# Block-local attention with routed experts: eight token rows to a partition, shared window rows copied inside SBUF, block means from sums and a product

## The chip, the cores and the metric

One core of a Trainium2 chip runs the whole program. The metric is the device time of one execution in microseconds; of several executions the median is taken. A profiled execution gives the trace: engine by engine, what ran when, what it waited for, and what the DMA engines moved.

## The reference

Two layers in sequence. The first is an attention over 4 x 8 heads, 768 tokens and 64 channels. Each query sees the keys less than 16 positions away, and 24 block summaries: for each block of 32 tokens the channelwise maximum of its keys and the mean of its values.

```python
k_sum = k.reshape(B, H, nb, block, D).max(axis=3)        # block = 32, nb = 24
v_sum = v.reshape(B, H, nb, block, D).mean(axis=3)
mask_l = np.abs(pos[:, None] - pos[None, :]) < window    # window = 16
scores_s = scale * np.einsum('bhsd,bhnd->bhsn', q, k_sum) + np.log(block)
scores_l_m = np.where(mask_l, scores_l, -1000000000.0)
scores_all = np.concatenate([scores_l_m, scores_s], axis=-1)
scores_all = scores_all - np.max(scores_all, axis=-1, keepdims=True)
a = np.exp(scores_all)
a = a / (np.sum(a, axis=-1, keepdims=True) + 1e-09)
v_all = np.concatenate([v, v_sum], axis=2)
return np.matmul(a, v_all).astype(np.float32)
```

The second layer sends each of the 3072 tokens, as a row of 512 channels, to the one of 8 experts with the largest gate logit: `relu(x @ w1[e]) @ w2[e]`, with 1024 hidden channels, times the gate's probability and a sigmoid. All inputs and outputs are float32.

## The kernel before, in words

**Attention tiles.** The work goes through 4 batches; a batch has 6 token tiles of 128 tokens, each of them two query blocks of 64 (`NB` = 12 in a batch), and a tile has two halves of the heads. That makes 48 stages `(b, tok, g)`. In a stage:

- `scores` multiplies each block's queries, for two heads at once, with a row of 120 columns (`W`): 48 keys before and in the block, 24 key maxima, 48 more keys. VectorE adds the mask and takes the minimum (L329), ScalarE the exponential (L331).
- `turn_p` transposes the weights on TensorE (L339) and copies them out.
- `values` multiplies them with a *window* `VW` of 120 rows (L350): 48 value rows, the 24 value means, 48 value rows, for all 8 heads, with a column of ones for the denominator. VectorE divides (L360), and POOL stores the tile to `x_dr`.
- `turn_x`, `logits`, `turn_logits` compute the gates; `route` (twice per batch) gives every token a place in its expert's list, with chains of small VectorE instructions (L402 to L446) and six scatters by POOL.

There are 9 window buffers (`VR`), used in turn.

**Preparation.** Queries and keys come in thirds of a batch: `load` brings 256 tokens of 8 heads, two token rows to a partition, so that a packet is 512 B. `reorder` copies the third so that a pair of heads is contiguous (L211 on VectorE, at the start also L209 on ScalarE); `transposed` turns it on TensorE (L273); `prep_k` and `prep_q` copy it from PSUM into `KT` and `QT` (L192), and `prep_k` takes the key maxima (L287), which `k_sum` spreads into the score rows (L296). `KT` holds a whole batch, twice; `QT` holds a third of one, twice, zeroed at the start by VectorE (L174), as half of it must be zero.

Value means: `load_vm` reads the values once more, 32 rows of 64 channels to a partition; `v_sum` adds them up (in the first batch L230 on VectorE, later L237 and L241 on POOL), `mean` scales them and POOL stores them to DRAM, from where `load_vsum` brings them into each window (L262). `load_vw` brings the value rows of two windows, in 256 B packets (L255, L256); neighbouring windows both load the 32 rows that they share.

**Order.** All of these loads go through SP's queue in the order that the code gives; the windows are loaded two token tiles ahead. The other engines' queues are ordered by a planner, which keeps to the order of the code where operands are ready. Before the first stage stand the memsets of the windows on POOL (L182), the first batch's keys, two thirds of its queries, its means and three token tiles' windows.

**Experts.** In the last batch the early experts' weights are fetched (L731), split into a high and a low part by ScalarE and VectorE (L733, L734), and multiplied in three products (L763 to L765, L852 to L854). Tokens are gathered from the lists by POOL (L712). This part begins near 200 us and runs to the end.

Of the kernel before, what the change touches and what calls it, by code (L numbers as in the profile page):

```python
# [20 lines left out]
P = 128  # L21
# [9 lines left out]
BUFS = {"sm": 4, "mn": 4, "pr": 4, "pT": 3, "xs": 3, "den": 3, "xT": 2, "ls": 2, "rawk": 3, "rawq": 2, "natk": 2, "natq": 2}  # L31
# [4 lines left out]
ON_DVE = ("p1", "lt", "ls")  # L36
RE = "vavavvv"
# [28 lines left out]
C_END = C_SEL + 2 * E  # L66


def constants():
# [20 lines left out]
    c[:, C_SEL:C_SEL + 2 * E] = p[:, None] % 32 == np.arange(2 * E)[None, :]  # L90
    return c
# [77 lines left out]
def attention(tc, const, sa, sb, st, ps, dr, q, k, v, id_sb, c_sb, wg_sb, x_dr, l_dr, rt, late_work):  # L169
    nc = tc.nc  # L170
    QT, KT, VW = [], [], []
# [8 lines left out]
    for i in range(VR):  # L180
        t = sb.tile([W, H, VP], F32, name=f"vw{i}", tag=f"vw{i}", bufs=1)
        nc.gpsimd.memset(t, 0.0)  # L182
        nc.gpsimd.memset(t[:, :, D:D + 1], 1.0)
        VW.append(t)
    def evac(what, dst, src, scale=None):
# [8 lines left out]
    vs_dr = dr.tile([B, H, NS, D], F32, name="vs_dr")  # L194
    raws, nat = {}, {}

    def load(kind, src, b, u):
        raw = (sa if kind == "k" else sb).tile([P, H, 2, D], F32, name=f"raw_{kind}{b}{u}", tag=f"raw{kind}",
                                               bufs=BUFS["raw" + kind])
        nc.sync.dma_start(  # L200
            raw.rearrange("p h j d -> p h (j d)"),
            src[b, :, 256 * u:256 * (u + 1), :].rearrange("h (p j) d -> p h (j d)", j=2))
        raws[kind, b, u] = raw

    def reorder(kind, b, u, engine="v"):
        t = (sa if kind == "k" else sb).tile([P, 2, H, D], F32, name=f"nat_{kind}{b}{u}", tag=f"nat{kind}", bufs=BUFS["nat" + kind])
        r = raws.pop((kind, b, u)).rearrange("p h j d -> p j h d")
        if engine == "a":
            nc.scalar.activation(t, r, AF.Copy)  # L209
        else:  # L210
            {"v": nc.vector, "p": nc.gpsimd}[engine].tensor_copy(t, r)  # L211
        nat[kind, b, u] = t

    vm = {}

    def load_vm(b, *os):
        for o in os:
            t = sa.tile([96, 32 * D], F32, name=f"vm{b}{o}", tag="vm", bufs=2)
            nc.sync.dma_start(t, v[b, 4 * o:4 * o + 4].rearrange("g (n s) d -> (g n) (s d)", n=NS))
# [720 lines left out]
```

## Time and profile before

| what | value |
|---|---|
| median of 3 runs (lowest to highest) | 564.43 us (563.89 to 564.97) |
| the profiled execution: time, span | 563.66 us, 561.8 us |
| busy: TensorE, VectorE, ScalarE, POOL | 500.7, 395.9, 339.1, 193.1 us |
| mean granted TensorE clock | 0.949 |
| DMA | 117.63 MB in 116799 packets, 53598 of them under 512 B |
| instructions | 12246 |

The span is what the trace covers, from the first to the last instruction; the time of the execution is 1.9 us longer. Lines such as L321 are lines of the kernel; `out<-in` are the program's names for what is written and read. An engine's busy time is an average over the attention and the experts, which have different limits. A number in brackets behind an instruction of the timeline is the idle time of its engine before it, and what ended it; "SPq" and "POOLq" are the queues of SP and POOL. Clock and DMA share are shown with 1.00 as full; the DMA share is the mean over 16 engines.

### The profile page before, as it was taken

The page shows a single profiled execution, that of the slowest core. Times are in us where ns is not written, and L with a number is a line of the kernel's source. Part 1 is how long each engine was busy: PE and PEld are TensorE (multiplying, and loading weights), DVE is VectorE, ACT ScalarE, POOL GpSimd, SP SyncE. Part 2 cuts the span into 40 slices and gives each one's busy share as a digit, 9 for nine tenths or more (in the row PEclk, how much of TensorE's full clock was granted, in tenths as well). Part 3 has the DMA queues.
Part 4 walks back from the last instruction along what each step waited for, and adds up shares of the span by engine and source line. Part 5 has one row for each costly group of instructions (what it writes and reads, how often), then busy time and mean ns, then how long its engine had stood idle before and what let it go on. Part 6 is the DMA issues. An engine that isn't in the chain of part 4 may idle for free. (4 is left out here: it accounts for less than half of the span.)

```text
span 561.8 us, 12246 instructions
## 1 busy us (share of the span) xinstructions
PE 500.7 (89%) x3880; PEld 436.5 (78%) x3880; DVE 395.9 (70%) x1210; ACT 339.1 (60%) x752; POOL 193.1 (34%) x222
## 2 busy tenths in 40 slices
PE   6498998988979789985999999999999999987990
PEld 5497786767768678874989989899898998975770
DVE  8878798759838857952767665776656666666892
ACT  4386786675749747442656554665555655547881
POOL 6036145445541420337643625415113031130111
PEclk8599998998979979997999999999999999998996
DMA  9979999999764874159667485774856737439790
GB/s 233 232 186 251 235 241 250 115 219 232 163 138 120 247 253 150 65 162 317 211 225 272 151 282 185 236 277 139 300 181 232 269 128 264 168 114 332 252 322 26
DMA packets 116799, 117.63 MB, mean 209 GB/s; under 512 B 53598, under 2 KB 78462, under 8 KB 115952
## 3 DMA queue, kind: packets, MB, share of 16 engines
q1 hardware_dynamic: 107584, 97.02, 61.3%
q0 software_dynamic: 9136, 19.69, 11.5%
q8 instruction: 34, 0.56, 0.5%
q14 instruction: 45, 0.37, 0.2%
HBM read 105.50 MB, written 13.79 MB: 212 GB/s over the span
## 5 line engine op out<-in xcount | busy, mean ns | idle before, releaser
L764 PE MATMUL hp<-xhl,w1h 128*128 128x256 f32 x384 | 109.0, 285 | 0.0
L765 PE MATMUL hp<-xhl,w1l 128*128 128x256 f32 x384 | 108.8, 284 | 0.0
L763 PE MATMUL hp<-xhl,w1h 128*128 128x256 f32 x384 | 108.4, 286 | 0.0
L733 ACT ACTIVATE w2h<-raw 128x512 fp32r<-128x512 f32 x104 | 64.7, 629 | 60.5 <-PE yp L854 27.7
L734 DVE TENSOR_TENSOR w2l<-raw,w2h 128x512 fp32r<-128x512 f32 x104 | 70.5, 689 | 35.2 <-ACT w2h L733 34.2
L852 PE MATMUL yp<-w2h,hh 128*128 128x512 f32 x216 | 87.3, 404 | 0.1
L853 PE MATMUL yp<-w2l,hh 128*128 128x512 f32 x216 | 85.4, 395 | 0.0
L854 PE MATMUL yp<-w2h,hl 128*128 128x512 f32 x216 | 85.2, 396 | 0.1
L331 ACT ACTIVATE pr<-sm,mn 128x120 f32<-128x120 f32 x192 | 62.1, 387 | 26.1 <-DVE mn L329 25.8
L763 PEld LDWEIGHTS hp<-xhl,w1h 128*128 128x128 f32 x384 | 73.7, 193 | 2.0 <-DVE w1l L734 0.4
L712 POOL DMA_INDIRECT xg<-x_dr,lst x28 | 32.3, 1152 | 124.5 <-PE xp L745 106.1
L764 PEld LDWEIGHTS hp<-xhl,w1h 128*128 128x128 f32 x384 | 74.1, 193 | 1.2 <-DVE xhl L748 0.2
L765 PEld LDWEIGHTS hp<-xhl,w1l 128*128 128x128 f32 x384 | 74.1, 193 | 0.0
L766 ACT ACTIVATE hh<-hp 128x256 fp32r<-128x256 f32 x96 | 36.5, 381 | 59.1 <-PE hp L765 57.0
L734 DVE TENSOR_TENSOR w1l<-raw,w1h 128x512 fp32r<-128x512 f32 x104 | 66.2, 690 | 7.3 <-ACT w1h L733 6.2
L767 DVE SCALAR_TENSOR_TENSOR hl<-hp,hh 128x256 fp32r<-128x256 f32 x96 | 39.6, 421 | 44.8 <-ACT hh L766 44.7
L321 PE MATMUL sp<-kt,qt 128*128 128x120 f32 x384 | 58.7, 301 | 7.9 <-DVE kt L296 7.0
L733 ACT ACTIVATE w1h<-raw 128x512 fp32r<-128x512 f32 x104 | 58.2, 621 | 6.9 <-DMA raw<-in_moe_w_dram 6.5
L321 PEld LDWEIGHTS sp<-kt,qt 128*128 128x128 f32 x384 | 53.8, 215 | 10.4 <-issue 8.3
L329 DVE CUSTOM_DVE_ANT_0 sm<-sp,c_sb 128x120 f32<-128x120 f32 x192 | 42.9, 277 | 14.6 <-PE sp L321 13.1
L854 PEld LDWEIGHTS yp<-w2h,hl 128*128 128x128 f32 x216 | 40.7, 189 | 9.5 <-DVE hl L823 0.5
L852 PEld LDWEIGHTS yp<-w2h,hh 128*128 128x128 f32 x216 | 41.2, 191 | 8.6 <-ACT hh L822 0.5
(285 smaller groups left out, 906.5 us busy)
## 6 DMA issues: line engine op xcount, KB each, us to landing
raw<-in_moe_w_dram SPq DMA_DIRECT2D x208, 256.0 KB
vw<-in_v_dram SPq DMA_DIRECT2D x88, 96.0 KB
raw_k<-in_k_dram SPq DMA_DIRECT2D x12, 512.0 KB
raw_q<-in_q_dram SPq DMA_DIRECT2D x12, 512.0 KB
vm<-in_v_dram SPq DMA_DIRECT2D x8, 768.0 KB
x_dr<-xs POOLq DMA_DIRECT2D x24, 256.0 KB, 5.8
vw<-vs_dr SPq DMA_DIRECT2D x36, 48.0 KB
vw<-in_v_dram SPq DMA_DIRECT2D x8, 64.0 KB
```

The source lines that it names most:

```text
L321: nc.tensor.matmul(sp[:, 2 * x + y, 0:W], lhsT=qt[:, 2 * g + x, li, :], rhs=kt[:, 2 * g + x, blk * KW:blk * KW + W], start=True, stop=True)
L329: nc.vector.tensor_tensor_reduce(out=sm[:, c, :], in0=sp[:, c, 0:W], in1=c_sb[:, m:m + W], scale=1.0, scalar=3.0e38, op0=ALU.add, op1=ALU. ...
L331: nc.scalar.activation(pr[:, c, :], sm[:, c, :], AF.Exp, bias=mn[:, c:c + 1], scale=-1.0)
L733: nc.scalar.activation(hi, raw, AF.Copy)
L734: nc.vector.tensor_tensor(lo, raw, hi.bitcast(F32), ALU.subtract)
L763: nc.tensor.matmul(hp, lhsT=w_h[:, fs], rhs=self.xh[:, c, :], start=c == 0, stop=False)
L764: nc.tensor.matmul(hp, lhsT=w_h[:, fs], rhs=self.xl[:, c, :], start=False, stop=False)
L765: nc.tensor.matmul(hp, lhsT=w_l[:, fs], rhs=self.xh[:, c, :], start=False, stop=c == NC - 1)
L767: nc.vector.scalar_tensor_tensor(hl[:, j, :], hp, 0.0, hh[:, j, :].bitcast(F32), ALU.max, ALU.subtract)
L852: nc.tensor.matmul(y, lhsT=hh[:, j, tk], rhs=w_h, start=j == 0, stop=False)
L853: nc.tensor.matmul(y, lhsT=hh[:, j, tk], rhs=w_l, start=False, stop=False)
L854: nc.tensor.matmul(y, lhsT=hl[:, j, tk], rhs=w_h, start=False, stop=j == NF - 1)
```

## The change

A unit is now one kind (key, query or value) of one pair of heads, all 768 tokens, eight token rows to each of 96 partitions: 12 units in a batch, 2 KB to a packet. Units are loaded five ahead of the stage and reordered two ahead, from the second batch on always by POOL. `QT` holds a whole batch, twice, and POOL zeroes its halves. Means: a unit of values is added up over its eight rows (three additions), and a product with a constant matrix `C_MEAN` adds four partitions and scales; the result stays in SBUF (`VS`). A window loads only the rows that its left neighbour does not hold; the shared 32 rows and the means are copied inside SBUF by `share_vw`, one token tile ahead. Key maxima are taken in two halves of a unit and joined where they are written into the score rows. The experts' code is the same. The last part of the diff, from `if g == 0` on, stands in the loop over the stages.

```diff
-BUFS = {"sm": 4, "mn": 4, "pr": 4, "pT": 3, "xs": 3, "den": 3, "xT": 2, "ls": 2, "rawk": 3, "rawq": 2, "natk": 2, "natq": 2}
+BUFS = {"sm": 4, "mn": 4, "pr": 4, "pT": 3, "xs": 3, "den": 3, "xT": 2, "ls": 2, "raw": 7, "nat": 4}
-ON_DVE = ("p1", "lt", "ls")
-RE = "vavavvv"
+ON_DVE = ("p1", "lt", "ls", "q11")
+T8 = 8
+G8 = S // T8
+RE = "vapvavvapvav"
+LOAD_AT, REORDER_AT = 5, 2
...
+    c[:, C_MEAN:C_MEAN + NS] = (p[:, None] // 4 == np.arange(NS)[None, :]) / 32.0
...
-        t = sb.tile([P, HP, 4, P], F32, name=f"qt{i}", tag=f"qt{i}", bufs=1)
-        nc.vector.memset(t, 0.0)
+        t = (sa, sb)[i].tile([P, HP, NB, P], F32, name=f"qt{i}", tag=f"qt{i}", bufs=1)
+        nc.gpsimd.memset(t[0:64, :, :, 64:P], 0.0)
+        nc.gpsimd.memset(t[64:P, :, :, 0:64], 0.0)
...
+    def load(kind, b, hp):
+        t = sa.tile([G8, 2, T8, D], F32, name=f"raw_{kind}{b}{hp}", tag="raw", bufs=BUFS["raw"])
+        nc.sync.dma_start(t.rearrange("p h j d -> p h (j d)"),
+                          {"k": k, "q": q, "v": v}[kind][b, 2 * hp:2 * hp + 2].rearrange("h (p j) d -> p h (j d)", j=T8))
+    def reorder(kind, b, hp, engine):
+        if kind == "v":
+            t = raw.rearrange("p h j d -> p h (j d)")
+            n = T8 * D
+            while n > D:
+                n //= 2
+                {"v": nc.vector, "p": nc.gpsimd}[engine].tensor_tensor(t[:, :, 0:n], t[:, :, 0:n], t[:, :, n:2 * n], ALU.add)
+        else:
+            t = sa.tile([G8, T8, 2, D], F32, name=f"nat_{kind}{b}{hp}", tag="nat", bufs=BUFS["nat"])
+            r = raw.rearrange("p h j d -> p j h d")
+            if engine == "a":
+                nc.scalar.activation(t, r, AF.Copy)
+            else:
+                {"v": nc.vector, "p": nc.gpsimd}[engine].tensor_copy(t, r)
+    def v_mean(b, hp):
+        mp = ps.tile([NS, 2, D], F32, name=f"vm{b}{hp}", tag="TR", bufs=PB["TR"])
+        nc.tensor.matmul(mp, lhsT=c_sb[0:G8, C_MEAN:C_MEAN + NS], rhs=nat.pop(("v", b, hp))[:, :, 0:D], start=True, stop=True)
+        evac("vs", VS[b % 2][:, 2 * hp:2 * hp + 2, 0:D], mp)
     def load_vw(b, tok):
-            lo = PAD if blk == 0 else 0
+            lo = PAD if blk == 0 else 2 * PAD
-    def load_vsum(b, tok):
+    def share_vw(b, tok):
         for blk in (2 * tok, 2 * tok + 1):
+            if blk:
+                nc.sync.dma_start(window(b, blk)[0:2 * PAD], window(b, blk - 1)[W - 2 * PAD:W])
             if blk < VR:
-                nc.sync.dma_start(VW[(NB * b + blk) % VR][LW:LW + NS, :, 0:D], vs_dr[b].rearrange("h n d -> n h d"))
+                nc.sync.dma_start(window(b, blk)[LW:LW + NS], VS[b % 2])
     def transposed(kind, b, hp, half):
+        for j in range(4):
+            nc.tensor.transpose(pt[:, j, :], t[:, 4 * half + j, :], id_sb[0:G8, 0:G8])
     def prep_k(b, hp, half):
+        for f in range(2):
+            d = kt[:, hp, PAD + 4 * half + 56 * f:PAD + 4 * half + 56 * f + (NB - 1) * KW]
...
+            evac(f"k{f}{half}", d, src[:, :, :, f, :])
+        nc.vector.tensor_reduce(out=km[b][:, hp, half, :], in_=pt.rearrange("p j (n s) -> p n s j", s=4), axis=AX.XY, op=ALU.max)
+        if half == 1:
...
+            nc.vector.tensor_tensor(own, m[0], m[1], ALU.max)
     def prep_q(b, hp, half):
+        for side in range(2):
...
+            evac(f"q{side}{half}", d, pt[r], -SCALE)
...
+    units = [(kind, b, hp) for b in range(B) for hp in range(HP) for kind in ("vkq" if b else "kqv")]
+    NU = 3 * HP
+    for i, u in enumerate(units[:NU]):
+        load(*u)
+        if i == 3:
+            load_vw(0, 0)
+    for i, (kind, b, hp) in enumerate(units[:NU]):
+        reorder(kind, b, hp, RE[i])
+        if kind == "v":
+            v_mean(b, hp)
+        else:
+            for half in range(2):
+                (prep_k if kind == "k" else prep_q)(b, hp, half)
     load_vw(0, 1)
+    share_vw(0, 0)
+    for u in units[NU:NU + LOAD_AT]:
+        load(*u)
+    for u in units[NU:NU + REORDER_AT]:
+        reorder(*u, "p")
...
         if g == 0:
+            if tok + 2 < TB or more:
+                load_vw(*divmod(b * TB + tok + 2, TB))
+            if tok + 1 < TB or more:
+                share_vw(*divmod(b * TB + tok + 1, TB))
+        for u in units[i + NU + LOAD_AT:i + NU + LOAD_AT + 1]:
+            load(*u)
+        for u in units[i + NU + REORDER_AT:i + NU + REORDER_AT + 1]:
+            second.append(lambda u=u: reorder(*u, "p"))
+        if more:
+            hp, x = divmod(step, 3)
+            if x < 2:
+                second.append(lambda: prep_k(b + 1, hp, x))
+            if x > 0:
+                second.append(lambda: prep_q(b + 1, hp, x - 1))
+            if x == 0:
+                second.append(lambda: v_mean(b + 1, hp))
```

More of the change, by code (lines that the diff above doesn't have):

```diff
@@ L184, in attention @@
         VW.append(t)
+    for i in range(2):
+        t = sb.tile([NS, H, VP], F32, name=f"vs{i}", tag=f"vs{i}", bufs=1)
+        nc.gpsimd.memset(t, 0.0)
+        nc.gpsimd.memset(t[:, :, D:D + 1], 1.0)
+        VS.append(t)
     def evac(what, dst, src, scale=None):
@@ L205, in reorder @@
[L205 to L209, printed above, removed]
-        else:
[L211 to L219, printed above, removed]
-            vm[b, o] = t
```

156 lines of the change are left out of this document (29 added, 127 removed).

## The prediction

> **What bounds the kernel now.** I read the page first, for engines and DMA, then the busy time by stretches.
>
> ```profile
> span 561.8 us, 12246 instructions
> PE 500.7 (89%) x3880; PEld 436.5 (78%) x3880; DVE 395.9 (70%) x1210; ACT 339.1 (60%) x752; POOL 193.1 (34%) x222
> DMA  9979999999764874159667485774856737439790
> GB/s 233 232 186 251 235 241 250 115 219 232 163 138 120 247 253 150 65 162 317 211 225 272 151 282 185 236 277 139 300 181 232 269 128 264 168 114 332 252 322 26
> DMA packets 116799, 117.63 MB, mean 209 GB/s; under 512 B 53598, under 2 KB 78462, under 8 KB 115952
> ```
>
> The share of busy TensorE time (89%) is an average over two stages. [...] The chain of waits reaches back only to 503 us, so it says nothing of the attention stage, the only one that is edited. So I cut that stage where the normalised outputs (L360) of a batch end:
>
> ```profile
> 26.00:65.00 39.00, 36.48 (x417) 31.90 (x416) 32.19 (x150) 29.44 (x78) 15.75 (x18) 0.95 0.93 219
> 65.00:108.50 43.50, 40.23 (x452) 34.04 (x451) 36.28 (x183) 31.34 (x85) 21.04 (x24) 0.96 1.00 204
> 108.50:158.80 50.30, 40.84 (x463) 34.26 (x461) 37.81 (x205) 32.00 (x86) 20.63 (x23) 0.97 1.03 202
> 158.80:210.40 51.60, 45.92 (x467) 39.15 (x468) 36.08 (x186) 35.20 (x89) 19.20 (x23) 0.87 0.66 192
> ```
>
> Columns: stretch, length, busy time and count of PE, PEld, DVE, ACT, POOL, granted clock, DMA share, GB/s. TensorE is busy for 40 to 41 us in the second and in the third batch, but the third takes 7 us longer, with DMA at its fullest. Nothing else is as busy as TensorE, so the stage is TensorE work plus holes. The largest hole lies between batches three and four:
>
> ```profile
> 154.00:168.00 14.00, 9.86 (x66) 8.77 (x64) 4.68 (x26) 5.64 (x14) 6.20 (x9) 0.76 0.69 145
> 168.00:182.00 14.00, 14.00 (x174) 12.57 (x171) 12.22 (x87) 13.31 (x41) 3.11 (x4) 1.00 0.41 109
> ...
> DVE nat_q L211 <- DMA raw_q<-in_q_dram: 6.3, 2, 4.0
> PE pv L350 <- DMA vw<-in_v_dram: 0.8, 1, 0.8
> ...
> 157.79 0.69 DVE L211 COPY nat_q<-raw_q 128x1024 f32<-128x1024 f32 x1 [3.98 <-DMA raw_q<-in_q_dram]
> 159.21 0.66 PE L369 MATMUL xtr<-id_sb,xs 128*128 128x128 f32 x4 [3.58 <-DVE ls L188]
> 163.06 2.75 PE L321 MATMUL sp<-kt,qt 128*128 128x120 f32 x12
> ```
>
> VectorE waits 3.98 us for queries; behind that copy stand the logits copy and TensorE, idle for 3.58 us. TensorE then runs at a lower granted clock (0.76 in this slice): 12 score matmuls take 2.75 us. A slice that holds 66 matmuls instead of 174 has lost 14 x (1 - 66/174) = 8.7 us.
>
> **The change, part by part.** The profiled execution took 563.66 us for its 561.8 us span; the median of the three runs is 564.43, 0.77 higher.
>
> *1. Loads, DMA waits.* Each partition row of a query or key load grows from 512 B to 2 KB, the 32 rows that two windows share come by a copy inside SBUF, 2304 B a row instead of eight times 256 B, and the means no longer go out to DRAM and back. Loads run five units ahead. I let the late query loads go: 8.7 us, of the other 2.3 of the 6.3 I count 1, and 0.8 for the window: -10.5. Ends: -7.1, if only the waits themselves go (6.3 + 0.8), though a wait that is hidden later gives back less, so -5; and -14, if the third batch also comes to the second's length (50.3 - 43.5 = 6.8, beside the 7 or so behind it). What is late next is the order of TensorE's queue, since it is busy for 40 of 43.5 us already.
>
> *2. The start.* Rows of the first 34 us, and prices:
>
> ```profile
> 1.21 2.62 SPq L200 DMA_DIRECT2D raw_k<-in_k_dram  x3
> 3.15 3.21 POOL L182 MEMSET vw<- 120x576 f32 x6
> 8.47 0.45 SPq L255 DMA_DIRECT2D vw<-in_v_dram  x1
> 24.42 2.03 PE L321 MATMUL sp<-kt,qt 128*128 128x120 f32 x8 [2.67 <-DVE kt L296]
> 29.62 2.48 SPq L262 DMA_DIRECT2D vw<-vs_dr  x6
> 33.78 0.45 PE L350 MATMUL pv<-vw,pT 120*64 120x65 f32 x4
> L677 POOL MEMSET xg<- 128x512 f32 x2 | 1.0, 562 | 0.0
> L107 POOL MEMSET wg_sb<- 128x128 f32 x1 | 0.2, 237 | 0.0
> GB/s 0 0 0 0 0 0 0 158 105 55 166 80 82 127 281 342 350 393 415 460 339 272 327 328 317 297 293 293 289 289 295 289 289 293 291 285 291 289 293 289
> ```
>
> (The last row is the DMA view of the first 10 us.) The zeroing of both query tiles goes from VectorE to POOL, ahead of the windows, as four memsets of 3072 elements a partition. The two POOL rows give 325 ns for 384 elements, so 0.85 ns each: 2.7 us a memset, 10.8 in all. The first window's memset, now at 3.15, moves to about 14, the second's to 14.6. SP's queue is in hand-written order: window loads of the first token tile stand behind four unit loads, and behind them the other eight. SP therefore waits until 14.6, and load five leaves at about 17. Eight units of 393 KB at the 290 GB/s of the row are 10.8 us, and the windows' 295 KB about 1.5: the last unit lands near 29. Then the value sum (1.4), the product with its copy (0.7), three copies inside SBUF (SP issues 0.45 each) and their landing (2; before, the last such copy is issued by 32.1 and used at 33.78): the first value product at 34.5, against 33.78. But the scores of the second half of the heads need query unit 3, which lands near 28, so they start at 31 instead of 26, and SP issues 5 more units (2 MB, 7 us) ahead of the third and fourth windows' copies, which holds the next values. I take +5. Ends: 0, if TensorE catches up in the first batch (it has the other queries ready); +9, if the 7 us are paid whole and the landing is 2 us later.
>
> *3. Engine work in the stage.*
>
> ```profile
> L273 PE MATMUL qtr<-id_sb,nat_q 128*128 128x128 f32 x96 | 16.0, 292 | 3.2 <-DVE den L359 2.0 <-ACT nat_q L209 0.9 <-ACT xT L192 0.2
> L211 DVE COPY nat_k<-raw_k 128x1024 f32<-128x1024 f32 x11 | 11.2, 1016 | 1.9 <-PE ktr L273 1.1 <-DMA raw_k<-in_k_dram 0.8
> L211 DVE COPY nat_q<-raw_q 128x1024 f32<-128x1024 f32 x11 | 8.2, 747 | 6.4 <-DMA raw_q<-in_q_dram 6.3
> L287 DVE TENSOR_REDUCE km<-ktr 128x16 f32<-128x512 f32 x24 | 16.1, 682 | 1.7 <-ACT kt L192 1.6
> L296 DVE COPY kt<-km 128x288 f32<-128x288 f32 x16 | 4.3, 305 | 0.1
> L192 ACT ACTIVATE qt<-qtr 64x512 f32<-64x512 f32 x48 | 28.3, 590 | 8.1 <-PE qtr L273 7.6
> L192 ACT ACTIVATE kt<-ktr 128x256 f32<-128x256 f32 x48 | 15.6, 382 | 7.5 <-PE ktr L273 7.3
> L237 POOL TENSOR_TENSOR vm<-vm 96x1024 f32<-96x1024 f32 x6 | 14.1, 2356 | 23.0 <-DMA vm<-in_v_dram 22.9
> L241 POOL TENSOR_TENSOR vm<-vm 96x512 f32<-96x512 f32 x6 | 8.1, 1355 | 0.3
> ```
>
> TensorE: behind the start stood 88 query and 72 key transposes; now 192, each of 96 columns, and 12 products. The whole group's 16.0/96 is 0.167 us. At 96/128 of that the transposes go from 26.7 to 24.0; at an unchanged price to 32.1; a product is two records of about that, 4 us for 12. So +1.3 to +9.4; I take +2.5, nearer the low end since the moving side shrinks with the columns. VectorE loses some 20 copies (15 us) and gains 12 joins of two half maxima (about 0.4 each, from L296), 12 query copies (q11, 0.5) and six more, shorter reductions: 5 us net of 142. It stood 23% idle, so half counts: -2.5, ends -5 and 0. ScalarE: 36 query copies of 384 elements (0.485, between the two L192 rows) and 48 key copies of 192 (0.33) and 12 of the means (0.28) are 36.7 us, against 44 x 0.59 + 36 x 0.382 = 39.7: 3 us less on an engine that waits for TensorE, so 0; without that cover -1.5.
>
> *4. POOL and the lock.*
>
> ```profile
> 129.36 2.35 POOL L237 TENSOR_TENSOR vm<-vm 96x1024 f32<-96x1024 f32 x1 [6.44 <-DMA vm<-in_v_dram]
> 129.38 2.39 DVE L404 TENSOR_TENSOR d<-lg,mx 128x48 f32<-128x48 f32 x1
> L404 DVE TENSOR_TENSOR d<-lg,mx x4: 199/206/2391, 83.1 to 226.1; 128x48 f32<-128x48 f32 x4
> 90.09 0.63 PE L273 MATMUL qtr<-id_sb,nat_q 128*128 128x128 f32 x4 [2.00 <-DVE den L359]
> ```
>
> A VectorE addition of two SBUF tensors, 0.2 us elsewhere, lasts 2.39 us and ends with POOL's addition. Routing has such a chain in each batch; at 90 us one costs TensorE 2.0 us. Every reorder of batches two to four is now POOL's: 24 copies of 1024 elements and 12 sums. A copy costs between the memset's rate (1.0 us) and the two-input L237 (2.36); I take 1.4, with one input. A sum is 1.36 for its first step and, by its shrinking size, 2.5 for three. Together 64 us in the 133 of three batches, against 14.1 + 8.1 and some 10 for the smaller steps before, in shorter pieces. Waits go with piece squared: 24 x 2.0 + 12 x 2.6 = 79, against about 50. The 4 us or so that TensorE lost become 6: +2. Ends: -3 (a piece never meets a chain) and +6 (copies at 2.36, and 12 new joins waiting). The x_dr issues stand on POOL between them, and as many scatters as before; nobody waits for either within a batch.
>
> [...]
>
> **Sum.** -10.5 + 5 + 2.5 - 2.5 + 2 = -3.5: 563.66 becomes 560.2, in terms of the median 560.9, say 561.
>
> **The rivals.** *B, slower:* SP waits for the windows' memset, as in 2, at its full +9, while part 1 gives only its -5 because the third batch is long for TensorE's order and not for DMA. With +2.5, -2.5 and +2 that is +6: 570. It decides when the last value unit lands after 34 us. For it: VectorE and TensorE hardly name DMA in the list of waits (6.3 and 0.8). Against: the 8.7 us hole has DMA at its head.
> *C, larger gain:* -14 in part 1, a start at +1, the rest +2: -11, 553. For it: the fourth batch loses its query preparation, and the first batch at DMA share 0.93 took 39 us. Against: POOL's doubled load.
> *D, no change:* each stage was hidden anyway; the hole's 8.7 is paid back by a start at +9: 565.
> *E, loads into 96 partitions are slower:* if the rate falls with the partitions, 96 of 128, to three quarters of the 290 GB/s, eight units take 14.5 us, the start costs 4 more: 565. [...] The trace does not settle it: the value loads were 96 wide, and shared the engines.
>
> **How the numbers follow.** Mine 0.41, B 0.24, C 0.18, D 0.08, E 0.09. A measurement can tell 0.2%, 1.1 us. My case alone, by half of its terms' ends, is 555 to 566. Faster: C, 0.37 of mine, 0.02 of E: 0.57. Same: D, 0.02 of mine, 0.04 of E: 0.14. Slower: B, 0.02 of mine, 0.03 of E: 0.29. The range reaches from C's 553, less 1, to B's 570.
>
> **What would show it.** The first window load on SP near 15 us and the first value product near 35 (part 2); no wait of VectorE or TensorE for a load after 50 us, and batch three near 43 us (1); VectorE under 36 us busy a batch (3); POOL copies near 1.4 us, and stretched VectorE additions beside them (4). I am wrong if POOL's memsets do not hold SP, if a key or query copy on POOL comes late for its transposes, or if the copies inside SBUF end a TensorE wait.

## The result, and the profile after

The median went from 564.16 us (562.79 to 564.97, 4 runs) to 633.57 us (631.75 to 636.45, 4 runs): a ratio of 1.1238, with a 95% interval of 1.1184 to 1.1291. The change costs 69 us, where the prediction had a gain of 3.5 and a range up to 570. The profiled execution has a span of 633.2 us, against 561.8. Some executions of a kernel are longer, at a lower TensorE clock (e5: 638.5 to 648.0 us at 0.871 to 0.876, beside 627.8 and 630.6 at 0.889 and 0.891); all ratios leave such ones out, and the trace of e5 below is of one and gives no times.

The page of the kernel after, its first two parts and its DMA rows, against those of the prediction:

```profile
span 633.2 us, 12638 instructions
...
PE 545.0 (86%) x3976; PEld 465.1 (73%) x3976; DVE 398.0 (63%) x1208; ACT 365.9 (58%) x786; POOL 225.9 (36%) x258
...
PEclk8557876597589879879989999999999999999997
DMA  4927991897298044785086775774774774656981
GB/s 123 211 39 172 238 211 46 178 223 159 80 208 206 18 108 107 166 302 185 2 288 235 265 244 160 253 258 160 262 262 153 254 268 136 223 177 195 317 303 61
DMA packets 85473, 118.06 MB, mean 186 GB/s; under 512 B 36254, under 2 KB 36414, under 8 KB 85392
```

Packets fell from 116799 to 85473, as intended; the bytes did not fall, since a copy inside SBUF counts too (44 of 72 KB for the shared rows and 36 of 54 KB for the means, 5.2 of the 118.06 MB). What is to be seen is the row of the DMA, whose slices are fortieths of the span: before, the engines were full in the first ten slices; now they have holes of 0.2 and less (slices of 39, 46 and 18 GB/s), and the granted TensorE clock falls to 0.5 and 0.6 in the same part. The stretches between the ends of the batches (columns as in the prediction), and below them the holes:

```profile
26.00:100.84 74.84, 55.07 (x446) 45.97 (x447) 36.92 (x170) 42.56 (x102) 26.93 (x33) 0.71 0.72 162
100.84:159.39 58.55, 53.34 (x486) 44.07 (x484) 37.62 (x182) 38.01 (x97) 24.76 (x29) 0.76 0.70 158
159.39:218.49 59.10, 51.14 (x482) 40.63 (x480) 41.34 (x204) 38.43 (x95) 24.74 (x30) 0.84 0.58 137
218.49:283.17 64.68, 53.20 (x498) 42.80 (x498) 38.99 (x184) 37.20 (x90) 20.88 (x25) 0.79 0.58 160
...
98.00:112.00 14.00, 11.81 (x62) 8.88 (x61) 4.95 (x17) 7.92 (x18) 2.58 (x3) 0.62 0.13 36
154.00:168.00 14.00, 12.15 (x70) 8.82 (x63) 6.40 (x15) 8.49 (x18) 8.95 (x11) 0.50 0.11 38
210.00:224.00 14.00, 10.34 (x92) 7.39 (x91) 10.48 (x55) 8.33 (x17) 8.19 (x9) 0.74 0.12 40
```

The attention ends at 283.2 us instead of 210.0: all of the loss is there. The first batch ends 36.2 us later (100.84 against 64.62), and the other three take 182.3 us instead of 145.4, 37.0 more. At each batch end stands a stretch of 14 us with some 60 to 90 matmuls, a clock of 0.50 to 0.74 and idle DMA. Before, the nearest to it was 154 to 168 us, where the DMA share was 0.69. TensorE seems busy in it (12 of 14 us), but 62 matmuls in 11.8 us are 190 ns each; at full clock (1.00, 168 to 182 us) and density the kernel before had 174 in 14 us, 80 ns each. From 140 to 168 us, where the clock falls to 0.50, the longest idle time of TensorE is 2.00 us; what lowers the clock is not shown.

The groups of instructions (out<-in, partitions x elements, count, busy us, mean ns of one, idle before and what ended it) of the kernel after:

```profile
L204 ACT ACTIVATE qt<-qtr 64x384 f32<-64x384 f32 x48 | 41.6, 866 | 8.0 <-PE qtr L268 7.5
L204 ACT ACTIVATE kt<-ktr 128x192 f32<-128x192 f32 x64 | 27.0, 533 | 26.8 <-PE ktr L268 26.7
L268 PE MATMUL ktr<-id_sb,nat_k 96*128 96x96 f32 x128 | 22.1, 318 | 8.0 <-DVE nat_k L230 3.5 <-DVE qt L202 3.1 <-ACT xT L204 1.0
L268 PE MATMUL qtr<-id_sb,nat_q 96*128 96x96 f32 x128 | 21.2, 308 | 14.8 <-ACT nat_q L228 11.0 <-ACT qt L204 2.1 <-DVE km L281 0.9
L202 DVE TENSOR_SCALAR qt<-qtr 64x384 f32<-64x384 f32 x16 | 13.7, 855 | 20.8 <-ACT qt L204 20.7
L230 POOL COPY nat_k<-raw_k 96x1024 f32<-96x1024 f32 x12 | 12.4, 1034 | 16.3 <-PE ktr L268 11.5 <-DMA raw_k<-in_k_dram 4.6 <-PE pt L327 0.2
L285 DVE TENSOR_TENSOR kt<-km 128x288 f32<-128x288 f32 x16 | 8.9, 558 | 0.4
L235 PE MATMUL vm<-raw_v,c_sb 96*24 96x128 f32 x32 | 8.2, 356 | 4.2 <-POOL raw_v L223 1.6 <-ACT qt L204 1.5 <-issue 1.2
L338 PE MATMUL pv<-vw,pT 120*64 120x65 f32 x768 | 42.9, 254 | 13.0 <-DMA vw<-vs 5.6 <-DMA raw<-in_moe_w_dram 4.2 <-DMA vw<-in_v_dram 2.0
```

Its waits (who waited for whom: us in total, times, longest):

```profile
SPq L258 <- ACT vs L204: 62.9, 4, 19.5
SPq L248 <- POOL vw L188: 12.4, 1, 12.4
...
POOL raw_v L223 <- DMA raw_v<-in_v_dram: 32.0, 12, 9.3
```

Two things stand out. The copies out of PSUM, which got a quarter smaller, became dearer: 866 ns for a query copy of 384 elements, where 512 took 590. And SP waits 62.9 us, four times for up to 19.5, for a mean (`vs`) before it may copy it into a window; every load behind it in SP's order waits too, then POOL for the loads.

### The profile page after: what moved, and what is told of

It reads as the page before. It is cut to its first block, busy times and chain, and to the rows that moved or that the text cites. A ratio compares the mean times of both kernels' runs of the same rounds, so it can differ in the third digit from the quotient of the medians.

```text
span 633.2 us, 12638 instructions
## 1 busy us (share of the span) xinstructions
PE 545.0 (86%) x3976; PEld 465.1 (73%) x3976; DVE 398.0 (63%) x1208; ACT 365.9 (58%) x786; POOL 225.9 (36%) x258
## 2 busy tenths in 40 slices
DMA packets 85473, 118.06 MB, mean 186 GB/s; under 512 B 36254, under 2 KB 36414, under 8 KB 85392
## 5 line engine op out<-in xcount | busy, mean ns | idle before, releaser
L696 ACT ACTIVATE w2h<-raw 128x512 fp32r<-128x512 f32 x104 | 64.6, 630 | 57.0 <-PE yp L817 27.3
L817 PE MATMUL yp<-w2h,hl 128*128 128x512 f32 x216 | 85.8, 399 | 0.2
L816 PE MATMUL yp<-w2l,hh 128*128 128x512 f32 x216 | 85.8, 397 | 0.0
L319 ACT ACTIVATE pr<-sm,mn 128x120 f32<-128x120 f32 x192 | 60.4, 382 | 37.1 <-DVE mn L317 36.9
L675 POOL DMA_INDIRECT xg<-x_dr,lst x28 | 31.6, 1127 | 121.0 <-PE xp L708 113.1
L309 PE MATMUL sp<-kt,qt 128*128 128x120 f32 x384 | 68.3, 330 | 7.3 <-DVE qt L202 7.3
L729 ACT ACTIVATE hh<-hp 128x256 fp32r<-128x256 f32 x96 | 36.5, 381 | 59.1 <-PE hp L728 57.0
L309 PEld LDWEIGHTS sp<-kt,qt 128*128 128x128 f32 x384 | 61.0, 239 | 10.8 <-DVE qt L202 8.2
L338 PE MATMUL pv<-vw,pT 120*64 120x65 f32 x768 | 42.9, 254 | 13.0 <-DMA vw<-vs 5.6
L223 POOL TENSOR_TENSOR raw_v<-raw_v 96x512 f32<-96x512 f32 (+2 forms) x42 | 34.6, 835 | 53.1 <-DMA raw_v<-in_v_dram 32.0
```

Source lines behind the costliest of these rows:

```text
L309: nc.tensor.matmul(sp[:, 2 * x + y, 0:W], lhsT=qt[:, 2 * g + x, blk, :], rhs=kt[:, 2 * g + x, blk * KW:blk * KW + W], start=True, stop=True)
L319: nc.scalar.activation(pr[:, c, :], sm[:, c, :], AF.Exp, bias=mn[:, c:c + 1], scale=-1.0)
L338: nc.tensor.matmul(po[64 * y:64 * y + 64, 2 * x + hh, :], lhsT=pT[:, 2 * x + y, 64 * hh:64 * hh + 64], rhs=VW[(NB * b + 2 * tok + y) % VR] ...
L696: nc.scalar.activation(hi, raw, AF.Copy)
L816: nc.tensor.matmul(y, lhsT=hh[:, j, tk], rhs=w_l, start=False, stop=False)
L817: nc.tensor.matmul(y, lhsT=hl[:, j, tk], rhs=w_h, start=False, stop=j == NF - 1)
```

## The experiments

Theory A at first: SP stops at the means, copies out of PSUM are too dear, and the start is late. The table gives, for each run, when the last normalised output of each batch was begun (from the traces, in us; for e2 and e4 without the last batch, which runs beside experts that get other tokens), and the ratio of its time to that of the kernel before on the same chip, with the interval.

| kernel | batch 1 | batch 2 | batch 3 | batch 4 | ratio |
|---|---|---|---|---|---|
| before | 64.6 | 108.1 | 158.4 | 210.0 | 1 |
| after | 100.8 | 159.4 | 218.5 | 283.2 | 1.1238 (1.1184 to 1.1291) |
| e1 row order | 94.2 | 145.7 | 203.2 | 263.4 | 1.0991 (1.0918 to 1.1065) |
| e2 means ready | 85.8 | 135.0 | 189.7 | | |
| e3 windows first | 94.7 | 150.0 | 209.1 | 275.0 | 1.1210 (1.1127 to 1.1293) |
| e4 = e1 + e2 | 80.2 | 131.9 | 185.9 | | |
| e5 means by ScalarE | | | | | 1.1056 (1.0978 to 1.1135) |
| e6 = e1 + e3 + e5 | 84.1 | 139.0 | 197.6 | 263.9 | 1.0908 (1.0835 to 1.0980) |
| e9 written order | 119.6 | 176.4 | 239.5 | 286.3 | 1.1358 (1.1299 to 1.1417) |
| e10 = e1 + e9 | 110.1 | 162.2 | 217.1 | 263.9 | 1.0956 (1.0884 to 1.1028) |
| e16 nine small tiles aside | 102.1 | 167.0 | 207.9 | 256.1 | 1.0817 (1.0749 to 1.0885) |
| e17 of these, the means' | 98.9 | 176.0 | 218.6 | 265.9 | 1.0956 (1.0892 to 1.1020) |
| e18 of these, the routing's | 113.2 | 166.7 | 228.2 | 281.2 | 1.1137 (1.1050 to 1.1223) |
| e11 = e1 + e16 | 95.8 | 158.8 | 198.8 | 246.3 | 1.0535 (1.0464 to 1.0607) |
| e12 = e1, means earlier | 96.8 | 146.9 | 206.3 | 271.6 | 1.1138 (1.1048 to 1.1228) |
| e13 = e11 + e12 + e3 | 91.0 | 146.3 | 190.2 | 240.6 | 1.0427 (1.0336 to 1.0518) |
| e14 = e13, loads first | 98.8 | 162.1 | 198.8 | 247.5 | 1.0556 (1.0477 to 1.0636) |
| e7 before, shared rows | 73.5 | 118.7 | 173.1 | 221.1 | 1.0110 (1.0057 to 1.0163) |
| e8 before, later reorder | 66.2 | 113.9 | 161.9 | 212.0 | 0.9951 (0.9907 to 0.9994) |
| e15 before, routing tiles aside | 66.8 | 110.6 | 156.3 | 208.8 | 1.0024 (0.9980 to 1.0068) |

**e1, the copies out of PSUM.** The changed kernel writes token `8r + j` of a query from row tile `j`, with `j` outermost, so that it writes every eighth element, 32 bytes apart. Here the four `j` of a half are innermost, and four elements in a row are written together:

```diff
-  d: [[1, 4], [P, NB], [T8, 8]]      # j, block, row   (keys likewise)
+  d: [[P, NB], [T8, 8], [1, 4]]      # block, row, j
```

> The changed kernel, with the copies out of PSUM into the key and query tiles walked the other way round: four neighbouring elements are written, then the next group, and the reads from PSUM take the stride. Theory A (the copies into every eighth element are slow, 866 ns a query copy and 533 ns a key copy, and hold the two PSUM buffers that all preparation goes through): a query copy falls to about 490 ns, a key copy to 330, and the time falls by 25 to 45 us, to 590 to 608. Theory B (SP's queue waits for the means and holds all loads behind it): the waits of about 15 us at each batch stay, and the time falls by less than 10 us. Theory C (POOL's memsets of the query tiles hold the first windows and all loads behind them): the copies get shorter and the time stays within 5 us.

The groups of e1 (columns as above):

```profile
L204 ACT ACTIVATE qt<-qtr 64x384 f32<-64x384 f32 x48 | 23.2, 482 | 11.0 <-PE qtr L268 10.4
L204 ACT ACTIVATE kt<-ktr 128x192 f32<-128x192 f32 x64 | 17.4, 324 | 25.4 <-PE ktr L268 24.9
L202 DVE TENSOR_SCALAR qt<-qtr 64x384 f32<-64x384 f32 x16 | 9.0, 561 | 10.0 <-ACT qt L204 9.8
```

866 became 482 ns, 533 became 324 and VectorE's 855 became 561, and the ratio fell from 1.124 to 1.099; the prices 485 and 330 that the prediction worked out were right for writes in this order. The order was the difference, at the same size and the same bytes. The gain in time, 2.5% or some 14 us, is less than the 25 to 45 us expected for it. In e1 the PSUM side is read 384 bytes apart instead, and that cost nothing visible (482 and 324 ns, against the 485 and 330 from copies of the kernel before).

**e2 and e4, means that are always ready; e3, the windows' memsets first.** In e2 the windows' means come from a constant tile, so SP does not wait; as the outputs then go to other experts, only the times of the attention can be compared.

```diff
# e2
-  nc.sync.dma_start(window(b, blk)[LW:LW + NS], VS[b % 2])
+  nc.sync.dma_start(window(b, blk)[LW:LW + NS], VC)
# e3: the four memsets of QT on POOL stand behind those of the windows
```

> The changed kernel, with the means' rows of the windows copied from a tile that is written once at the start, so that these copies wait for no preparation; the true means are still computed, and not used. Theory B: SP's four waits of together 63 us go, loads run ahead again, and the time falls by 35 to 55 us, to 580 to 600. Theory A: the preparation is as slow as before, TensorE waits for it and not for SP; the time falls by 5 to 15 us. Theory C: no change beyond 5 us.

> The changed kernel, with POOL's four memsets of the query tiles behind those of the windows. Theory C: the first window load leaves SP near 6 us instead of 15.5, and the whole time falls by about 9 us, to 624. Theory A and theory B: the start is bound by the preparation of all four pairs of heads, or by the wait for the means behind it; the time falls by 0 to 4 us.

> Both the other walk of the copies and the means' rows from a tile that is always ready. If A and B are two separate costs, the savings of the two single runs add up, within 5 us. If they are one chain (slow copies make the means late, and the late means hold SP), the sum is larger than the joint saving by 10 us or more.

At the end of batch three e1 gains 15.3 us, e2 28.8, e4 32.6. The two overlap by 11.5: both shorten one chain, from a copy out of PSUM to the next product and on to SP. e3 gains 9.4 us there, but its ratio is not told apart from the changed kernel's. And even e4 stays 27.5 us behind the kernel before: SP's wait and the dear copies are not all of it. In e13, which has POOL's memsets in this order too, VectorE's first four key copies, beside them, take 2.31 us in the mean instead of 1.07, which fits a price that this order has of its own.

**e5 and e6, the means by ScalarE's queue.** Here the means stay true and SP is out of it:

```diff
-  nc.sync.dma_start(window(b, blk)[LW:LW + NS], VS[b % 2])
+  nc.scalar.dma_start(window(b, blk)[LW:LW + NS], VS[b % 2])
```

> The copies of the means into the windows (36 of them) are issued by ScalarE's queue, where the copy that makes a mean also stands, and no longer by SP; nothing else is edited. Theory A (SP's queue, which is in hand-written order, stops at a mean that is not there yet, and all loads behind it start late): the loads run on, the 36th normalised output comes at 193 to 205 us instead of 218.5, and the time is 606 to 620 us. The start gains little, since the last mean of the first batch is still ready only at 48 us. Rival B (the means are late for the value products by whichever queue they come): the 36th output stays within 4 us of 218.5 and the time at 628 to 638 us.

> The row order of e1 (adjacent rows innermost in the copies out of PSUM), the window memsets ahead of the query tiles' of e3, and the means on ScalarE's queue, together. Theory A (a head of line on SP, strided copies and a late start are separate parts of one chain, and what is left is more TensorE work in the preparation): 36th output at 180 to 192 us, time 590 to 605 us, still slower than before by 25 us or more. Rival B (means late by any queue): no more than the two single results give, 36th output near 195 to 200 and 612 to 618 us. Rival C (nothing but these three): the time comes back to 565 to 575 us.

e5 gains 1.8%, between its two forecasts, and e6 is hardly better than e1 alone (1.091 against 1.099, intervals overlapping). Rival C of e6 falls, and theory A has lost most of its ground: with copies, means and memsets repaired, batches still take 55 to 66 us. What came out is rival B of e6 (batch three ends at 197.6 us, where it had 195 to 200): the means are late by whichever queue they are copied.

**e9 and e10, TensorE in written order.** In the changed kernel's trace the planner sends a batch's scores ahead and leaves the next batch's preparation to its end. Theory F was that this is the harm.

```diff
-  with tc.manual_schedule(engines={SP}):
+  with tc.manual_schedule(engines={SP, PE}):
```

> The changed kernel with TensorE in written order in the attention stage, as SP is, and not in the planner's; no instruction is added, removed or edited. Theory F (the planner sends scores, turns and values of a batch ahead and piles the preparation of the next batch up at the batch's end, where it goes in series through two PSUM buffers with TensorE at a low clock): the preparation spreads, so the slow stretches at 98 to 126 and 154 to 186 us go, and the 36th normalised output comes at 185 to 205 us instead of 218.5; the time is 600 to 620 us, less the harm of a written order in the last batch. Rival A (the stops are SP's, at the means): they stay, in a written order too, 36th output over 212 us.

> Written order on TensorE in the attention stage together with e1's row order (adjacent rows innermost in the copies out of PSUM). Theory F: 36th output at 172 to 192 us (e1 alone 203.2), time 585 to 605 us. Rival A: no more than e1 alone, 36th output over 198 us and ratio to the kernel before near 1.10.

Theory F falls as it was forecast: e9 is slower than the changed kernel, e10 no faster than e1. In e10 the stretches of low clock at 98 and 154 us do go (1.00 from 90 to 120 us and from 150 to 170), but the second and third batch, where F had the gain, change by 4 us or less in e9 and e10. Written order lengthens the first batch by 16 to 19 us and shortens the fourth, which prepares nothing, by 13 to 18; why is not shown. The second batch of e10, in which the work is spread out and the clock is 0.93, takes as long as e1's second (51.5, at the same clock):

```profile
110.13:162.22 52.09, 44.35 (x483) 37.34 (x482) 35.97 (x181) 30.86 (x95) 26.92 (x32) 0.93 0.76 178
```

**e11, and e16 to e18: the pair of PSUM buffers.** Transposed keys, queries and outputs, the means' products, the logits, the turned logits and the two rank tiles of the routing all go through the two buffers of one tag (`TR`). The change raises their number in a batch from 26 to 34: 8 key and 8 query tiles instead of 6 and 6, and 4 products. A buffer is free only when the last copy out of it is done. Theory G: this pair sets the pace. In e16 the nine small tiles go to the value products' pair; nothing else differs from the changed kernel. e17 and e18 move the means' four and the routing's five alone, and e11 is e16 on top of e1.

```diff
-  mp = ps.tile([NS, 2, D], F32, name=f"vm{b}{hp}", tag="TR", ...)
+  mp = ps.tile([NS, 2, D], F32, name=f"vm{b}{hp}", tag="PV", ...)   # e17; lt, rk, tot: e18
```

> e1 (row order), and besides the products of the means, the turned logits and the two rank tiles leave the pair of PSUM buffers that the transposes of keys, queries and outputs go through, for the pair of the value products. The shared pair then serves about 25 tiles a batch (before the change 26, after it 34). Theory G (that pair, filled and emptied in series, sets the pace of a batch): the period of a batch falls from e1's 52 to 57 us to 45 to 50, the 36th output comes at 183 to 193 us instead of 203.2, time near 595 to 608 us. Rival A (the pace is set by SP's stops at the means and by more TensorE work): the 36th output stays within 4 us of 203, the time within 0.7% of e1's ratio of 1.099.

> The changed kernel with only the small tiles moved (the products of the means, the turned logits, the rank tiles), the row order as it was. Theory G: the 36th output comes at 190 to 203 us instead of 218.5, ratio to before 1.07 to 1.09 instead of 1.124; less than that if the strided copies were what made the pair slow (then it gains mostly with the row order, as in e11), ratio 1.10 to 1.12.

> The changed kernel, with only the products of the means moved to the value products' pair of PSUM buffers (4 of the 34 tiles a batch); the turned logits and rank tiles stay. Theory A' (what e16 gained is that a mean no longer queues behind the preparation in that pair, so that SP is released sooner): nearly all of e16's gain, ratio 1.08 to 1.095, SP's waits for the means near 26 us instead of 62.9. Theory G' (it is the routing's tiles that wait behind, and hold, the preparation): little, ratio 1.11 to 1.125.

> The changed kernel, with only the turned logits and the rank tiles moved (5 of 34 tiles a batch); the means stay. Theory A': little, ratio 1.105 to 1.125, SP's waits for the means over 50 us. Theory G': most of e16's gain, ratio 1.08 to 1.095.

e16 brings the ratio from 1.124 to 1.082, e11 from e1's 1.099 to 1.054: 4.2 and 4.6%, from a change of tags. No other single edit gains as much time. Two thirds of it come with the four means' tiles (e17, 2.8%); for the routing's tiles (e18, 1%) the intervals overlap. That is theory A' more than G', and SP's waits for the means went with it: 23.5 us in e17, 49.5 in e18. The gain is in the third and fourth batch: from the end of batch two on, the changed kernel needs 123.8 us, e16 89.2 (256.13 - 166.98) and the kernel before 101.9. The second batch got no shorter (64.9 against 58.6 us), so the times expected at the end of the third are missed (207.9, not 190 to 203, and 198.8 in e11, not 183 to 193), while the ratio of e16 came out as expected and that of e11 slightly better. Waits of SP in e16:

```profile
SPq L258 <- ACT vs L204: 26.5, 2, 16.7
```

Its four waits for a mean (62.9 us) have become two, though nothing on SP was edited: a mean no longer queues for a buffer behind a batch's keys and queries.

**e12, e13 and e14.** e12 makes the last mean two steps sooner and lets SP copy it one step later, so that SP should not wait, while the pair stays as it was.

```diff
# e12: value unit 4 of the next batch one place sooner, its mean at step 7 instead of 9;
#      the copies of the means one step later, behind that step's loads
# e14: at the start, five loads of the second batch ahead of the copies of the means
```

> e1, and besides the last value unit of the next batch is taken one place sooner, its mean is made at step 7 and not 9, and SP copies the means into a window one step later, behind the loads of that step: four steps, some 16 us, lie between a mean and its copy instead of one. Theory A (SP's stop at the means holds the loads): no SP wait for the means after the start, DMA share over 0.6 at the batch ends, 36th output at 186 to 196 us instead of 203.2, time 598 to 610 us. Rival G (the PSUM pair sets the pace): SP's waits go but the period stays at 52 to 57 us and the time within 0.7% of e1's ratio.

> e11 and e12 together, with e3's order of the memsets besides. If both theories hold: 36th output at 170 to 182 us, time 580 to 595 us. If neither does: 36th near 198 us, 613 to 618 us.

> e13, and at the start SP issues the five unit loads of the second batch ahead of its copies of the first batch's means, so that it does not hold them while it waits 14 us for the means (24 to 38 us in e13, DMA share 0.02 from 30 to 40). Theory A (what is left of the loss is the start, and it is SP's stop there): the 12th output comes 6 to 14 us sooner than e13's 90.95, the time is 10 us or so less, ratio to before near 1.025. Rival H (the start is bound by the preparation of all twelve units ahead of the first value product, whoever loads): 12th output within 3 us of 90.95, ratio near 1.043.

SP's waits for a mean in e1 and in e12:

```profile
SPq L258 <- ACT vs L204: 45.8, 4, 15.8
SPq L260 <- ACT vs L204: 23.9, 4, 15.3
```

They fell as low as in e16 and e17, and the time did not fall with them: 1.114 against e1's 1.099. So SP's stop alone does not set the pace, and the tile in the pair has a part. How much of e17's gain is the tile's and how much SP's is not told apart, since e17 changes both and e12 moves the mean's product and a load besides. With the pair relieved, e13 is the best of the changed kernels, 1.043. Its batches:

```profile
26.00:90.95 64.95, 53.47 (x507) 43.91 (x506) 37.05 (x174) 38.38 (x113) 29.57 (x36) 0.83 0.71 169
90.95:146.32 55.37, 45.93 (x476) 39.10 (x476) 34.31 (x180) 31.06 (x93) 27.04 (x33) 0.85 0.73 167
146.32:190.22 43.90, 39.21 (x482) 33.62 (x484) 36.12 (x204) 31.63 (x94) 22.27 (x28) 0.98 0.74 178
190.22:240.63 50.41, 45.26 (x474) 39.80 (x473) 35.82 (x177) 29.37 (x77) 17.86 (x22) 0.88 0.70 204
```

Batches two to four now take 149.7 us, against 145.4 before and 182.3 in the changed kernel: of their 37.0 us of loss, 32.7 are found. What is left is the first batch, which ends at 91.0 instead of 64.6. e14 lets SP load five units through its wait there, and the first batch ends no sooner (98.8). So it is not these loads; the copies of the means themselves leave SP 6 us later than in e13 (44.23 against 38.03). Rival H, that twelve units have to be prepared ahead of the first value product, does not fit e13 either: there the last mean of the first batch is copied out of PSUM by 38 us, and the first value product comes only here:

```profile
56.87 0.40 PE L236 MATMUL vm<-raw_v,c_sb 96*24 96x128 f32 x2
57.20 1.15 PE L341 MATMUL pv<-vw,pT 120*64 120x65 f32 x32
```

It stands right behind the first mean of the *second* batch, which in the order of the code comes ahead of it and now goes through the same pair. It is so in e11, e16 and e17 too (0.3 to 0.6 us behind, at 62 to 68 us), and not in e18, where the means stayed in `TR` and the first value product comes at 50.64, as in the changed kernel (50.47). So moving the means has a price at the start, and 4.2% is what e16 gains net of it. In e14 the first value product comes at 51.09, and still the first batch ends later than in e13: that is not all of it, and what is left of the first batch stays open.

**Parts of the change on the kernel before: e7, e8, e15.**

```diff
# e7: load_vw starts at row 2 * PAD; one token tile later:
+  nc.sync.dma_start(VW[(NB*b + blk) % VR][0:2 * PAD], VW[(NB*b + blk - 1) % VR][W - 2 * PAD:W])
# e8: reorder("q") one token tile after its load
# e15: lt, rk, tot from tag TR to PV
```

> The kernel before, with one part of the change alone: of each window the 32 rows that it shares with the one ahead are copied inside SBUF by SP, one token tile later, instead of being loaded. Keys, queries, means and their order stay as they were. Theory A (these copies are not what costs): 560 to 567 us, a gain at most where 32 of 96 packets of a window go. Rival D (a copy inside SBUF makes SP wait for the load of the window ahead, and the loads behind it stand): 36th output over 162 us instead of 158.4, time over 569 us.

> The kernel before, where the copy that reorders a query load is issued one token tile (two steps, some 7 us) after its load instead of in the same step, so that VectorE does not stand in front of a load that has not landed. Theory A (the 8.7 us hole between batches three and four is this late query load, as the prediction has it): the hole shrinks and the time is 555 to 561 us. Rival E (the hole has another head, and the query wait only fills it): 562 to 567 us, with another wait at 154 to 168 us.

> The kernel before, with the turned logits and the two rank tiles moved from the pair of PSUM buffers of the transposes to the pair of the value products; nothing else. Theory G (the pair sets the pace wherever it is loaded): 1 to 3% faster than before, 550 to 560 us at a time before near 564. Rival: before, with 26 tiles a batch through the pair, another thing bounds (TensorE's work and the loads), within 0.5% of no change.

e7: the shared rows alone cost 1.1%, some 6 us, as its rival D had it; the attention ends 11 us later than before (221.1 against 210.0), and SP waits 9.3 us, in three pieces, for a load to land before it issues such copies (`SPq L262 <- DMA vm`). e8: more than half of the hole that the prediction built on goes. The same stretch as in the prediction, which had 66 matmuls there:

```profile
154.00:168.00 14.00, 12.73 (x126) 10.49 (x124) 9.69 (x50) 8.17 (x20) 5.39 (x7) 0.88 0.91 150
```

The wait for queries (6.3 us) is down to 0.5, 60 more matmuls lie in these 14 us, and the time hardly falls: by 0.5% (0.1 to 0.9%) by the ratio, some 3 us, and not at all by the medians of all executions (569.8 and 569.6 us). e15 does nothing that can be told: with 26 tiles a batch the pair did not bind. No version beats the kernel before by more than e8 does.

## Why the prediction was wrong

**Part 1 (-10.5).** Batches two to four got 37.0 us longer instead. Two steps failed. A hole of 8.7 us was put down to the late query load and counted as 8.7 us of gain; e8 takes that wait away, and by the prediction's own formula 3.9 us of the hole stay (14 x (1 - 126/174)), while the time falls by 3 at most. And "loads run five units ahead" holds for the code, not for SP: the lead is spent when SP stands at the copies of the means, 62.9 us in all. I had priced these copies (0.45 us to issue, 2 to land) and never asked when their source is ready and what is queued behind them. No wait of VectorE or TensorE for a load after 50 us was forecast; TensorE waits 2.0 us for a window's value rows (L338, ending at 150.65), POOL, which does the reorders now, 32.0 for value units, and the third batch took 59.1 us, not 43.

**Part 2 (+5, ends 0 and +9).** SP's queue and TensorE's work at the start, in the timeline of the kernel after (start, length):

```profile
15.51 0.31 SPq L248 DMA_DIRECT2D vw<-in_v_dram  x1
17.36 0.47 SPq L211 DMA_DIRECT2D raw_q<-in_q_dram  x1
27.06 0.31 SPq L211 DMA_DIRECT2D raw_v<-in_v_dram  x1
28.90 0.43 SPq L249 DMA_DIRECT2D vw<-in_v_dram  x1
48.11 0.94 SPq L258 DMA_DIRECT2D vw<-vs  x1
...
33.47 1.05 PE L235 MATMUL vm<-raw_v,c_sb 96*24 96x128 f32 x4 [1.57 <-POOL raw_v L223]
34.45 1.54 PE L268 MATMUL ktr<-id_sb,nat_k 96*128 96x96 f32 x8
36.89 1.58 PE L268 MATMUL qtr<-id_sb,nat_q 96*128 96x96 f32 x8 [0.90 <-DVE km L281]
39.64 0.59 PE L235 MATMUL vm<-raw_v,c_sb 96*24 96x128 f32 x2 [1.18 <-issue]
40.59 1.67 PE L268 MATMUL ktr<-id_sb,nat_k 96*128 96x96 f32 x8 [0.36 <-ACT vs L204]
44.66 1.00 PE L268 MATMUL qtr<-id_sb,nat_q 96*128 96x96 f32 x8
47.12 0.40 PE L235 MATMUL vm<-raw_v,c_sb 96*24 96x128 f32 x2 [1.47 <-ACT qt L204]
50.47 0.48 PE L338 MATMUL pv<-vw,pT 120*64 120x65 f32 x2 [0.38 <-DMA vw<-vs]
```

The mechanism that I saw is there to within a microsecond: the first window load at 15.51 (forecast 14.6 to 15), load five at 17.36 (17). The step that failed is the end of the chain. I let the last unit land at 29 and added its sum, product and copies: 34.5. The last load was issued only at 27.06, because a raw buffer had to come free, and landed at 34.7 (VectorE begins to add it up at 34.69, after a wait for it). From then on the units went one after another through the pair of PSUM buffers, each waiting for the copies of the one ahead: 6.2 and 7.5 us from one mean to the next, 13.7 from 33.47 to 47.12. The first value product came at 50.47, and the first batch ended 36 us late.

**Part 3 (+2.5, -2.5, 0).** Sizes, and a resource left out. Query and key copies were put at 0.485 and 0.33 us and cost 0.866 and 0.533, for the order of their writes (e1). Transposes of 96 columns were put at 96/128 of the old 0.167 us. They cost 0.169 ((22.1 + 21.2)/256) at the changed kernel's lower clock (0.883) and 0.148 in e13 (0.924), a tenth less and not a quarter (the first line is of the kernel before, the others of e13):

```profile
L273 PE MATMUL ktr<-id_sb,nat_k 128*128 128x128 f32 x96 | 15.6, 296 | 5.2 <-DVE nat_k L211 3.1 <-ACT xT L192 1.0 <-ACT qt L192 1.0
L271 PE MATMUL ktr<-id_sb,nat_k 96*128 96x96 f32 x128 | 19.5, 291 | 15.3 <-DVE nat_k L231 11.4 <-ACT xT L205 2.2 <-DVE km L284 1.4
L271 PE MATMUL qtr<-id_sb,nat_q 96*128 96x96 f32 x128 | 18.5, 286 | 4.5 <-DVE km L284 3.5 <-DVE ls L201 0.7 <-ACT qt L205 0.2
```

Keys, queries and means together keep TensorE busy for 51.5 us (22.1 + 21.2 + 8.2), before for 31.6 (15.6 and 16.0): 19.9 more over the kernel, where the term's high end was 9.4 behind the start. VectorE, put at 5 us less, is busy for 2.1 us more over the whole kernel (398.0 against 395.9), and for 36.9 to 41.3 us a batch where under 36 was forecast. "ScalarE waits for TensorE, so 0" turned round: VectorE's and TensorE's work now waits for ScalarE's copies (20.7 us for L202 alone). And the two `TR` buffers, whose relief in e16 is worth 4.2%, stand in no term, though 26 and 34 tiles could be counted in the code.

**Part 4 (+2).** Nothing speaks against it, but no run takes this term alone. A POOL copy takes 1.034 us, where 1.4 was taken and 1.0 was the lower bound. The joins of L285 take 0.558 us in the mean, where 0.4 was put for them: 0.458 in the median, and 1.966 at the longest (at 161.17 us, beside a POOL copy of 1.05). That POOL's work holds VectorE's, the lock in the name of this part, is an estimate from such pairs: the traces show the two side by side, not the cause.

**The rivals.** B had the sign. Its mechanism, SP behind the windows' memset, is in the trace (12.4 us), but e3 takes that wait away, ends the first batch 6.1 us sooner and gains 0.3% in all, which can't be told from nothing. So B was right on the sign mostly for a reason that was not the cause, though its condition came true: the last value unit landed after 34 us. E is borne out in part. From 5 to 9.4 us the changed kernel loads almost nothing but units, 96 partitions wide, at 247 GB/s with full DMA engines (share 1.05); from 6 to 10 us the kernel before had 293 (share 1.20). That is 0.84 of the rate, where E had three quarters, and makes eight units 12.7 us instead of 10.8. Whether it comes from the partitions is not shown, since the packets changed as well. Of the three conditions named for being wrong, one came true plainly: copies of the means inside SBUF end 5.6 us of TensorE's waits at L338, and the loads that they held end more.

What the runs show of the 69 us: moving the nine tiles out of the pair gives back 4.2% of the time before (with SP's shorter waits, and net of the later start), the order of the writes another 2.8% (e11 against e16), order of means and memsets about 1% (e13 against e11, intervals overlapping), and 4.3% that remain in e13, most of it in the first batch. The shares of single edits overlap and don't add up by themselves.

## What to carry to other kernels

Count what goes through each small ring of buffers, PSUM's above all, before and after: more and smaller tiles in the same two buffers can cost more than everything that the change was priced by (here 4.2%, e16 against the changed kernel). When a value that used to come from memory is now computed, ask when it is ready, who waits for it in a hand-written queue, and what stands behind that wait. Moving a tile to another ring puts it in line with that ring's users: look at what now stands behind it. A hole in the trace is an upper bound of a gain: work that moves up meets the next limit (in e8, 4.8 of the 8.7 us went and the time fell by 3 at most).

## What the runs showed of the hardware that was not expected

- Writing float32 into SBUF with 32 bytes between neighbours cost ScalarE 866 instead of 482 ns for 64 x 384 elements and 533 instead of 324 for 128 x 192, and VectorE 855 instead of 561 (the changed kernel against e1); reading PSUM 384 bytes apart instead cost nothing that shows (482 and 324 ns in e1, where 485 and 330 had been worked out from the kernel before).
- A float32 transpose of 96 by 96 took TensorE 0.148 us in the mean (e13, clock 0.924), one of 128 by 128 0.165 (31.6/192, the kernel before, clock 0.949): a tenth less for three quarters of the columns.
- Larger packets did not make the loads the faster: units 96 partitions wide in 2 KB packets moved at 247 GB/s (the changed kernel, 5 to 9.4 us), loads of 512 B packets, in part 128 partitions wide, at 293 GB/s (the kernel before, 6 to 10 us), with the DMA engines full in both (shares 1.05 and 1.20).
- The granted TensorE clock fell to 0.50 from 154 to 168 us in the changed kernel, in a stretch in which TensorE counts as busy for 12.15 of 14 us.
